# Moving batch 3's loads around batch 2's DMA transpose, and one weight quarter ahead of a load of q

## The chip, the cores and the metric

The kernel runs on one core of one Trainium2 chip. The metric is device time in microseconds (us) of one execution. A verdict calls two kernels the same when they are within 2%; it is unclear when the interval of the ratio reaches past 2%. A run counts as fast when it is at most 1.5% above the fastest of its kernel.

Engines: PE (TensorE matmul), PEld (TensorE weight load), DVE (VectorE), ACT (ScalarE), POOL (GpSimd), SP (SyncE). SP computes nothing here: it issues DMAs, in the traces one after the other in program order. PSUM is the memory into which PE writes.

## The reference, cut to what matters

```python
# q, k, v: (8 batches, 8 heads, 576 positions, 64), float32
q_s = softmax(q over its 64);  k_s = softmax(k over the 576 positions)
kv  = einsum('bhsd,bhse->bhde', k_s, v)           # per head 64 x 64
x   = einsum('bhsd,bhde->bhse', q_s, kv)          # -> 4608 tokens x 512
h   = x @ w_in                                    # 512 -> 2048
out = (h * sigmoid(h)) @ w_out                    # 2048 -> 512
```

The 4608 tokens go through the two large matmuls in 9 chunks: `mm1` (512 to 2048, 16 steps a chunk) and `mm2` (2048 to 512, 16 steps a chunk, four for each quarter of w_out). Attention of the next batch is woven in between: exp and row sum of q, transpose of q, the product `kv`, and `xt`, which multiplies the transposed q by `kv`.

## The kernel before

The order in which each engine gets its instructions is the order in which the Python code makes them. A list of units, one `mm1` or `mm2` step each, is walked, and `plan(u, f)` runs f just before unit u. The traces show SP's issues and DVE's instructions in this order.

```python
def load(b, name, src, ccs=None, eng=nc.sync):       # q, k or v of one batch: 1.18 MB, issued by SP
    ...                                              # two buffers for each of qt, kt, vt
    eng.dma_start(out=st[b][name][:, c, :], in_=x[:, c, :])

def tr_dma(b, eng):                                  # transpose of the normalized exp(q), by DMA
    eng.dma_start_transpose(out=qt_tile(b)..., in_=st[b]["eq"]...)

def kvcopy(b, cc):                                   # DVE: kv / column sums -> kvn; frees kv's PSUM tiles
    ...
def xt(t, cc, ...):                                  # PE: needs kvn (DVE) and qT (the DMA transpose)
    ...

# loads on the GpSimd queue, at the start
load_w1(0); load_w1(1); load_w2(0); load_w1(2)
load(1, "qt", q, eng=nc.gpsimd)
load_w2(1)                                           # second quarter of the output weights
load_w1(3)
load(1, "kt", k, eng=nc.gpsimd); load_w2(2); load(1, "vt", v, eng=nc.gpsimd); load_w2(3)
# ... cut: batch 0 ...

def plan_attn(b, u, sm, vs, tp, ks, ox, eng=nc.gpsimd):
    for cc in range(2):
        plan(u + sm[cc], lambda cc=cc: exp(b, "qt", "eq", cc))                        # ACT
        plan(u + sm[cc] + 1, lambda cc=cc: (qsum(b, cc), qnorm(b, cc, nc.gpsimd)))    # DVE, then POOL
    for cc in range(2):
        plan(u + sm[2 + cc], lambda cc=cc: exp(b, "kt", "ek", cc))
        plan(u + vs[cc], lambda cc=cc: vcast(b, cc, eng))
    plan(u + tp, lambda: tr_dma(b, nc.sync))
    if b == 1:
        plan(u + vs[0] + 1, lambda: load_behind(2))  # q, k, v of batch 2
    if b + 2 < B:
        at_ = u + max(tp, vs[1]) + 1
        plan(at_, lambda: [load(b + 2, *x) for x in (("qt", q), ("kt", k), ("vt", v))])
    # ... cut: kv, kvcopy and xt at ks and ox ...

plan_attn(1, begin[1], (-20, -19, -11, -10), (-6, -5), -12, (-4, -3), (-2, 0), V)
plan_attn(2, begin[2], (-23, -21, -18, -15), (-13, -12), -15, (-10, -7), (-5, -3))
for b in range(3, B):
    plan_attn(b, begin[b], (-40, -36, -32, -28), (-34, -30), -20, (-15, -11), (-7, -4))
```

The softmax here doesn't subtract the row's maximum and nothing guards it: scores larger than these inputs give would overflow.

## Time and profile before

| | before |
|---|---|
| time, median of 3 runs | 292.98 us (292.74 to 295.19) |
| span of the profiled run | 291.8 us |
| PE busy | 279.4 us, 96% |
| DVE, ACT, POOL busy | 53%, 52%, 18% |

From the page: busy time of PE (us, share of the span, instructions), and the granted TensorE clock in 40 slices of 7.3 us (9 is 90% or more of full speed).

```profile
PE 279.4 (96%) x1970; PEld 130.4 (45%) x1970; DVE 153.3 (53%) x308; ACT 152.6 (52%) x250; POOL 52.0 (18%) x44
...
PEclk9999999998899999999999999999999999999998
```

PE is the bottleneck, so only its own idle or slow time is worth anything. The longest of PE's waits (what waited, for what, total us, times, longest) are:

```profile
PE o_1076 L179 <- DMA qT<-eq: 2.1, 1, 2.1
PE wps L302 <- DVE warm L258: 1.2, 1, 1.2
PE ops L233 <- DMA W_59<-in_moe_w_out_dram: 0.9, 1, 0.9
PE o_1077 L179 <- DVE kvn_64 L158: 0.8, 1, 0.8
```

Two of the four are one place. Here is PE's timeline around it (start, duration, engine, line, what, count; in brackets the idle time before and what ended it):

```profile
67.86 0.24 PE L179 MATMUL o_1076<-qT,kvn_63 64*64 64x128 bf16 x2
68.92 0.24 PE L179 MATMUL o_1077<-qT,kvn_63 64*64 64x128 bf16 x2 [0.82 <-DVE kvn_64 L158]
71.28 0.53 PE L179 MATMUL o_1076<-qT,kvn_64 64*64 64x384 bf16 x2 [2.12 <-DMA qT<-eq]
...
71.75 1.89 PE L233 MATMUL ops<-W_59,GT 128*128 128x512 bf16 x4
73.43 1.47 PE L198 MATMUL hps<-XT,W_58 128*128 128x448 bf16 x4
```

At `xt` of batch 2, PE waits 0.82 us for kvn and then 2.12 us for the transposed q. The next four matmuls of 512 columns take 1.89 us where others take 1.03. The windows view tells why (us, then busy time and instruction count of PE, PEld, DVE, ACT, POOL; granted clock; share of DMA; GB/s). The clock is 0.83 on average over these 10 us; the clock records in the trace say 0.5 for 3.41 us, from 71.1 to 74.5.

```profile
70.00:80.00 10.00, 8.72 (x43) 3.59 (x43) 3.30 (x5) 5.84 (x9) 2.94 (x3) 0.83 0.98 340
```

Why is the transpose late? From POOL's timeline and SP's:

```profile
56.74 4.19 POOL L103 TENSOR_TENSOR eq<-eq,rzq 128x1152 bf16<-128x1152 bf16 x2 [21.84 <-DVE rzq L98]
...
46.31 0.46 SPq L74 DMA_DIRECT2D qt<-in_q_dram  x1
46.86 2.55 SPq L74 DMA_DIRECT2D kt<-in_k_dram  x1
49.46 2.76 SPq L74 DMA_DIRECT2D vt<-in_v_dram  x1
52.27 14.00 SPq L252 DMA_DIRECT2D out_dram<-ost  x8
66.38 3.23 SPq L114 DMA_TRANSPOSE qT<-eq  x1
```

The transpose's input is ready at 60.93, when POOL ends. But SP issues it at 66.38. In front of it stand the three loads of batch 3 (here) and of batch 2 (just before), and eight stores. Their issues do not take their usual half microsecond: k and v take 2.55 and 2.76 us and the stores 14 us, because SP is held until about the time when an earlier load lands: k's issue ends at 49.41, and q of batch 2 is reported landed at 49.82. The last load lands at 65.79. The transpose lands at 71.24, and PE starts at 71.28.

The 0.8 us for kvn has another cause: DVE is busy with a row sum of batch 3 (1.35 us) that stands in front of batch 2's kvn in its list.

```profile
66.81 1.35 DVE L97 TENSOR_REDUCE zq<-eq 128x18 f32<-128x1152 bf16 x1
68.58 0.28 DVE L158 TENSOR_SCALAR kvn_64<-kvps,rz 128x64 bf16<-128x64 f32 x1
```

### The profile page before, as it was taken

The numbers are of one execution on the slowest core, as the hardware profiler recorded it, in microseconds if no ns is written. First come the engines' busy times: TensorE is split into PE (matmuls) and PEld (weight loads), VectorE is DVE, ScalarE is ACT, GpSimd is POOL, SyncE is SP. The second block draws the span as 40 slices with busy tenths as digits, with TensorE's granted clock in tenths as the row PEclk, the third lists the DMA queues.
The fourth block names the chain that finished last, engine by engine and source line by source line (L and its number), as shares of the span: only waits on it lengthen the run. The fifth ranks groups of instructions, "written<-read, shape, count | busy, mean of one in ns | idle before, by whom it ended". The sixth has DMA issues, their size and how long they took to land.

```text
span 291.8 us, 4982 instructions
## 1 busy us (share of the span) xinstructions
PE 279.4 (96%) x1970; PEld 130.4 (45%) x1970; DVE 153.3 (53%) x308; ACT 152.6 (52%) x250; POOL 52.0 (18%) x44
## 2 busy tenths in 40 slices
PE   8899899995999999999999999999999999999992
PEld 3466554442444444444444444444444444444440
DVE  3985754855454565546554655465453444345431
ACT  5675555853663576357635863486325433553330
POOL 0740500262320035003500250025000000000000
PEclk9999999998899999999999999999999999999998
DMA  7999999998949903991299228001800240023006
GB/s 276 289 199 289 315 232 324 392 391 194 395 106 201 398 30 74 197 400 46 63 184 376 92 52 173 2 1 43 185 2 0 49 97 0 0 67 80 0 0 144
DMA packets 38311, 46.39 MB, mean 159 GB/s; under 512 B 18064, under 2 KB 22160, under 8 KB 38288
## 3 DMA queue, kind: packets, MB, share of 16 engines
q1 hardware_dynamic: 33248, 38.35, 45.1%
q0 software_dynamic: 5040, 7.73, 11.8%
q8 instruction: 15, 0.25, 0.4%
q14 instruction: 8, 0.07, 0.1%
HBM read 36.70 MB, written 9.44 MB: 158 GB/s over the span
## 4 chain that ended last, share of the span: by engine, by line
PE 75%; DMA 21%; SPq 1%; POOL 1%; issue 0%; DVE 0%; ACT 0%
PE ops L233 38%; PE hps L198 34%; DMA W_59<-in_moe_w_out_dram 11%; DMA vt<-in_v_dram 8%; DMA qT<-eq 2%; PE kvps L145 2%; POOL W_58 L274 1%; SPq L74 1%; DVE ost L246 0%; PE o_1076 L179 0%; ACT XT L190 0%; SPq L252 0%; PE o_3057 L179 0%; PE o_3033 L179 0%; PE o_2142 L179 0%
## 5 line engine op out<-in xcount | busy, mean ns | idle before, releaser
L214 DVE SCALAR_TENSOR_TENSOR GT<-sg,hps 128x512 bf16<-128x512 f32 (+2 forms) x176 | 99.7, 584 | 120.7 <-ACT sg L206 119.9
L233 PE MATMUL ops<-W_59,GT 128*128 128x512 bf16 x576 | 147.7, 381 | 1.1 <-DMA W_59<-in_moe_w_out_dram 0.9
L198 PE MATMUL hps<-XT,W_58 128*128 128x512 bf16 (+3 forms) x640 | 147.5, 359 | 0.5 <-DVE XT L188 0.2
L206 ACT ACTIVATE sg<-hps 128x512 f32<-128x512 f32 (+3 forms) x160 | 87.8, 554 | 108.8 <-PE hps L198 104.2
L198 PEld LDWEIGHTS <-W_58 128*128 128x128 bf16 x640 | 62.1, 98 | 66.0 <-issue 3.5
L233 PEld LDWEIGHTS <-GT 128*128 128x128 bf16 x576 | 54.8, 98 | 64.2 <-issue 3.8
L103 POOL TENSOR_TENSOR eq<-eq,rzq 128x1152 bf16<-128x1152 bf16 x14 | 29.6, 2118 | 137.2 <-ACT sg L206 99.5
L97 DVE TENSOR_REDUCE zq<-eq 128x18 f32<-128x1152 bf16 x16 | 21.5, 1346 | 4.1 <-ACT eq L83 4.1
L83 ACT ACTIVATE eq<-qt 128x1152 bf16<-128x1152 f32 x16 | 18.5, 1164 | 2.4 <-DMA qt<-in_q_dram 2.4
L83 ACT ACTIVATE ek<-kt 128x1152 bf16<-128x1152 f32 x16 | 18.5, 1158 | 1.0 <-DMA kt<-in_k_dram 1.0
L248 ACT ACTIVATE ost<-ops 128x512 f32<-128x512 f32 x18 | 10.7, 597 | 9.9 <-PE ops L233 8.8
L246 DVE TENSOR_SCALAR ost<-ops 128x512 f32<-128x512 f32 x18 | 12.3, 685 | 5.4 <-PE ops L233 5.4
L302 PE MATMUL wps<-warm 128*128 128x512 bf16 x32 | 10.1, 471 | 1.2 <-DVE warm L258 1.2
L145 PEld LDWEIGHTS <-ek 64*64 64x64 bf16 x576 | 6.2, 107 | 7.1 <-issue 3.8
L90 POOL CAST vaug_61<-vt 128x1152 bf16<-128x1152 f32 x6 | 6.8, 1160 | 0.0
L90 POOL CAST vaug_60<-vt 128x1152 bf16<-128x1152 f32 x6 | 6.8, 1157 | 0.0
L302 PEld LDWEIGHTS <-warm 128*128 128x128 bf16 x32 | 3.5, 116 | 6.1 <-issue 3.3
L157 DVE RECIPROCAL rz<-kvps 128x1 f32<-128x1 f32 x32 | 5.0, 157 | 0.1
L98 DVE RECIPROCAL rzq<-zq 128x18 f32<-128x18 f32 x16 | 4.3, 266 | 0.9
L145 PE MATMUL kvps<-vaug_60,ek 64*64 64x65 bf16 x288 | 4.0, 194 | 0.4 <-ACT vaug_60 L88 0.4
L145 PE MATMUL kvps<-vaug_61,ek 64*64 64x65 bf16 x288 | 3.8, 194 | 0.1
L158 DVE TENSOR_SCALAR kvn_63<-kvps,rz 128x64 bf16<-128x64 f32 x12 | 3.4, 284 | 0.4
(135 smaller groups left out, 74.8 us busy)
## 6 DMA issues: line engine op xcount, KB each, us to landing
out_dram<-ost SPq DMA_DIRECT2D x72, 128.0 KB, 2.3
qt<-in_q_dram SPq DMA_DIRECT2D x6, 1152.0 KB, 6.0
kt<-in_k_dram SPq DMA_DIRECT2D x6, 1152.0 KB, 9.3
vt<-in_v_dram SPq DMA_DIRECT2D x6, 1152.0 KB, 11.6
W_58<-in_moe_w_in_dram POOLq DMA_DIRECT2D x4, 512.0 KB, 9.7
W_59<-in_moe_w_out_dram POOLq DMA_DIRECT2D x4, 512.0 KB, 19.3
qt<-in_q_dram SPq DMA_DIRECT2D x2, 576.0 KB, 4.0
kt<-in_k_dram SPq DMA_DIRECT2D x2, 576.0 KB, 6.8
```

The source lines that it names most:

```text
L83: nc.scalar.activation(out=o, in_=jgd(st[b][src], cc), func=ACT.Exp)
L90: eng.tensor_copy(o, jgd(st[b]["vt"], cc))
L97: nc.vector.reduce_sum(out=st[b]["zq"][:, cc], in_=e, axis=AX.X)
L103: eng.tensor_tensor(out=e, in0=e, in1=r[:, :, :, None].to_broadcast([128, J, 2, D]), op=ALU.mult)
L145: nc.tensor.matmul(out=t[r][g * 64:(g + 1) * 64, 0:E1], lhsT=st[b]["ek"][r * P:(r + 1) * P, j, G * D:(G + 1) * D], rhs=vaug[b % 2][r * P:( ...
L198: nc.tensor.matmul(out=hps[:, 0:size], lhsT=W1[:, c, fb * 128:(fb + 1) * 128], rhs=XT[t][:, c, off:off + size], start=(c == 0), stop=(c == ...
L206: nc.scalar.activation(out=sg[:, 0:size], in_=hps[:, 0:size], func=ACT.Tanh, scale=0.5)
L214: nc.vector.scalar_tensor_tensor(out=GT[g][:, fb, col:col + n], in0=sg[:, h], scalar=1.0, in1=hps[:, h], op0=ALU.add, op1=ALU.mult,)
L233: nc.tensor.matmul(out=OP[t, tb], lhsT=GT[t][:, fc, tb * 128:(tb + 1) * 128], rhs=W2[:, fc, :], start=(fc == 0), stop=(fc == NFB - 1),)
L246: nc.vector.tensor_scalar_mul(out=ost, in0=OP[t, tb], scalar1=0.5)
L248: nc.scalar.activation(out=ost, in_=OP[t, tb], func=ACT.Copy, scale=0.5)
L302: nc.tensor.matmul(out=wps, lhsT=warm[:, 0:128], rhs=warm, start=True, stop=True)
```

## The change

The intent: the loads of batch 3 are begun around batch 2's transpose (q in front, k and v behind it) instead of all in front; batch 3's exponentials and row sums come later, to match; the second quarter of the output weights goes ahead of q of batch 1 on the GpSimd queue, to remove the wait of 0.9 us.

```diff
     load_w1(2)
+    load_w2(1)
     load(1, "qt", q, eng=nc.gpsimd)
-    load_w2(1)
     load_w1(3)
@@ plan_attn
-        if b + 2 < B:
-            at_ = u + max(tp, vs[1]) + 1
-            plan(at_, lambda: [load(b + 2, *x) for x in (("qt", q), ("kt", k), ("vt", v))])
+        else:
+            x = (("qt", q), ("kt", k), ("vt", v))
+            if b + 1 == 3:
+                plan(u + tp - 3, lambda: load(3, *x[0]))
+                plan(u + tp + 1, lambda: [load(3, *y) for y in x[1:]])
+            if b + 2 < B:
+                plan(begin[3] - 31 if b == 2 else u + tp + 1, lambda: [load(b + 2, *y) for y in x])
@@
-    plan_attn(1, begin[1], (-20, -19, -11, -10), (-6, -5), -12, (-4, -3), (-2, 0), V)
-    plan_attn(2, begin[2], (-23, -21, -18, -15), (-13, -12), -15, (-10, -7), (-5, -3))
-    for b in range(3, B):
+    plan_attn(1, begin[1], (-18, -17, -11, -10), (-6, -5), -12, (-4, -3), (-2, 0), V)
+    plan_attn(2, begin[2], (-23, -21, -18, -15), (-14, -13), -15, (-10, -7), (-5, -3))
+    plan_attn(3, begin[3], (-36, -33, -28, -25), (-27, -24), -20, (-15, -11), (-7, -4))
+    for b in range(4, B):
         plan_attn(b, begin[b], (-40, -36, -32, -28), (-34, -30), -20, (-15, -11), (-7, -4))
```

What this does to SP's list: before, it read "three loads of batch 3, eight stores, transpose, three loads of batch 4". Now it reads "eight stores, q of batch 3, transpose, k and v of batch 3, three loads of batch 4". Planning batch 4's loads at a later unit changes nothing: nothing else of SP stands between the two places. One detail of the diff: the casts of v of batch 2 come one unit earlier.

## The prediction

> **What bounds the kernel now.** TensorE: 279.4 of 291.8 us busy (busy times), and the chain of waits is 75% PE. From 76 us to the end it runs without a stall, so only the first 76 us can give anything. There the list of waits and the timeline show: 0.89 us at 29.0 for the second quarter of the output weights (landed 29.88); 0.25 us at 37.5 for the third quarter (landed 37.49); about 0.25 us at 43.7 for the fourth (landed 43.71); and a hole at batch 2's output product: 0.82 us at 68.1 for kvn, because DVE stands in batch 3's 1.35 us row sum, then 2.12 us at 69.2 for the transposed q of batch 2, issued at 66.38 and landed at 71.24. Right after that hole the granted clock is 0.5 for 3.41 us (71.1 to 74.5), where matmuls of 512 columns start 427 ns apart instead of 216: about 1.65 us more. The Trainium skill ("TensorE: Matmul & The Clock Gate", section on the HAM clock gate) says that an idle window of about 3.4 us halves the clock; the trace agrees (about 2.9 us idle of the 3.4 before it, then 3.41 us at half).
>
> **Why the transpose is late.** Its input was ready at 60.9 (last GpSimd normalization). But the sync queue holds six 1.18 MB loads in front of eight stores in front of it. Their issues block (2.5, 2.8 us) and the stores until 66.3; the last load lands only at 65.79.
>
> **What the change does.** No instruction is added or removed. The stores and q of batch 3 now stand in front of the transpose, k and v behind it. Loads of batch 2 should land as now (49.8, 52.8, 55.8), the stores by about 58, q of batch 3 by about 61. The transpose is then issued at about 61 and lands 4.7 to 4.9 us later, near 66, before its use at 67.7. The row sum of batch 3 moves behind kvn. So 0.8 + 2.1 + 1.65 us and small gaps vanish: today the stretch from 67.86 to 75.17 takes 7.3 us, without stalls its matmuls need 2.4 us. Gain 4.9 us, all on the critical path.
>
> k and v of batch 3 should land by about 69 and 72, before their use at about 76; batch 4's loads by about 81.
>
> **The weight quarter.** It should land at about 26, and the wait of 0.89 us at 29 vanishes. But the third quarter's place in the GpSimd queue is unchanged, so it still lands at about 37.5; PE arrives there earlier and waits about 1.2 us. That gain is given back: at most 0.2 us net, from the fourth quarter. q of batch 1 lands near 29.5, its transpose is issued near 37 instead of 34.93 and should still land near 45, just in time for its use at 46.
>
> I subtract 0.3 us for small new ring stalls.
>
> **Predicted:** 292.98 - 4.9 - 0.2 + 0.3 = 288.2 us, range 286.8 to 290.0. Faster by over 2%: 0.13; within 2%: 0.84; slower: 0.03.
>
> **Right if** the wait for the transposed q of batch 2 is gone, the transpose is issued near 61, the granted clock has no half-speed stretch near 71, and the wait for weights moved from 29 to about 36.5 to 37.5 with nearly the same total. **Wrong if** the third quarter lands earlier too (then up to 1 us more, near 2%), if batch 1's transpose lands after 46 (a new wait of up to 2 us, perhaps a half-speed stretch), if the stores still block the sync queue past 61, or if k of batch 3 comes too late for its exponential.

## The result, and the profile after

The changed kernel took 289.5 us (median of 6 runs, 288.79 to 289.9) against 293.94 us for the kernel before (6 runs, 292.74 to 295.21). The ratio is 0.9846, 95% interval 0.9811 to 0.9881. A ratio is the mean time of one kernel's fast runs over that of the other's of the same rounds, so it is not quite the ratio of the medians. In later rounds on one chip (run e10 below) it was 0.9823 (0.9799 to 0.9848). So the gain is 1.5 to 1.8%, clear of noise. The first comparison puts it under 2%; the interval of e10 just reaches 2%, and the recorded verdict there is unclear.

PE's waits in the changed kernel, all of those of 0.6 us or more:

```profile
PE ops L233 <- issue: 1.7, 11, 0.2
PE kvps L145 <- ACT vaug L88: 1.5, 2, 0.8
PE wps L302 <- DVE warm L258: 1.2, 1, 1.2
PE ops L233 <- DMA W<-in_moe_w_out_dram: 1.1, 1, 1.1
PE qtps L126 <- DVE eq L103: 0.6, 1, 0.6
```

The waits for qT and for kvn in the middle are gone. The first line is not a stall: this trace has 1936 matmul records of 1970, and where one is missing a gap of 0.2 us shows. The lines of `kvps` and `qtps` belong to batch 0, before 16 us. The wait for the output weights is still there, as large as before or larger. PE's timeline at the same `xt`, the windows, and SP's timeline:

```profile
68.72 0.41 PE L179 MATMUL o<-qT,kvn 64*64 64x128 bf16 x8
69.29 0.81 PE L233 MATMUL ops<-W,GT 128*128 128x512 bf16 x3 [0.16 <-issue]
69.94 0.92 PE L198 MATMUL hps<-XT,W 128*128 128x448 bf16 x4
70.79 0.41 PE L179 MATMUL o<-qT,kvn 64*64 64x128 bf16 x8
71.13 1.04 PE L233 MATMUL ops<-W,GT 128*128 128x512 bf16 x4
```

```profile
70.00:80.00 10.00, 9.95 (x54) 4.51 (x54) 6.05 (x10) 7.85 (x13) 5.73 (x4) 1.00 1.05 397
```

```profile
47.80 9.62 SPq L252 DMA_DIRECT2D out_dram<-ost  x8
57.52 0.54 SPq L74 DMA_DIRECT2D qt<-in_q_dram  x1
61.82 3.21 SPq L114 DMA_TRANSPOSE qT<-eq  x1
65.12 0.53 SPq L74 DMA_DIRECT2D kt<-in_k_dram  x1
```

The transpose is issued at 61.82, just after POOL's last normalization ends (61.79), so its input sets the time of the issue now, not the loads in front of it in SP's list. It lands at 66.51, and PE needs it at 68.72. On DVE, the row sum of batch 3 no longer stands in front of kvn, whose last part ends at 68.53, also in time. There is no half clock. The stretch from the first matmul of `xt` to the `mm2` step after its second half lasts 71.13 - 68.72 = 2.41 us; before it was 75.17 - 67.86 = 7.31 us. That is 4.90 us.

Outside this stretch the two profiled runs differ by little. From its end to the end of the span it is 216.7 us in both. Before it, the changed kernel is 0.86 us later (68.72 against 67.86). Most of that is chance of the run: the last load of batch 0 landed at 12.70 us against 12.06, before anything that the change touches. 4.90 - 0.86 is 4.04, the difference of the spans (4.0).

### The profile page after: what moved, and what is told of

Its sections match the earlier page's. It is cut to its first block, busy times and chain, and to the rows that moved or that the text cites. A ratio compares the mean times of both kernels' runs of the same rounds, so it can differ in the third digit from the quotient of the medians.

```text
span 287.8 us, 4948 instructions
## 1 busy us (share of the span) xinstructions
PE 273.3 (95%) x1936; PEld 129.5 (45%) x1970; DVE 153.2 (53%) x308; ACT 152.0 (53%) x250; POOL 52.0 (18%) x44
## 4 chain that ended last, share of the span: by engine, by line
PE 82%; DMA 10%; POOL 2%; issue 1%; DVE 1%; SPq 0%; ACT 0%; ACTq 0%
PE ops L233 40%; PE hps L198 38%; DMA W<-in_moe_w_out_dram 8%; DMA vt<-in_v_dram 3%; PE kvps L145 2%; PE o L179 2%; POOL W L274 1%; POOL W L280 1%; DVE ost L246 0%; SPq L74 0%; DVE GT L214 0%; POOL kt L74 0%; POOL qt L74 0%; DVE vaug L90 0%; ACT XT L190 0%
## 5 line engine op out<-in xcount | busy, mean ns | idle before, releaser
L198 PE MATMUL hps<-XT,W 128*128 128x512 bf16 (+3 forms) x633 | 146.4, 358 | 1.2 <-DVE XT L188 0.3
L233 PE MATMUL ops<-W,GT 128*128 128x512 bf16 x550 | 143.0, 379 | 3.6 <-issue 1.7
L198 PEld LDWEIGHTS <-W 128*128 128x128 bf16 x640 | 61.9, 98 | 65.8 <-issue 2.8
L190 ACT CAST XT<-o 128x512 bf16<-128x512 f32 (+3 forms) x36 | 18.4, 565 | 6.5 <-PE o L179 6.5
L90 POOL CAST vaug<-vt 128x1152 bf16<-128x1152 f32 x12 | 13.5, 1159 | 0.0
L302 PE MATMUL wps<-warm 128*128 128x512 bf16 x31 | 8.8, 440 | 1.2 <-DVE warm L258 1.2
L158 DVE TENSOR_SCALAR kvn<-kvps,rz 128x64 bf16<-128x64 f32 x32 | 9.1, 284 | 1.1
L145 PE MATMUL kvps<-vaug,ek 64*64 64x65 bf16 x576 | 7.8, 194 | 1.6 <-ACT vaug L88 1.5
L179 PE MATMUL o<-qT,kvn 64*64 64x320 bf16 (+7 forms) x128 | 7.7, 296 | 0.4 <-DVE kvn L158 0.3
L179 PEld LDWEIGHTS <-kvn 64*64 64x64 bf16 x128 | 2.6, 104 | 7.6 <-issue 4.6
```

The lines of the kernel that those rows point to most:

```text
L90: eng.tensor_copy(o, jgd(st[b]["vt"], cc))
L145: nc.tensor.matmul(out=t[r][g * 64:(g + 1) * 64, 0:E1], lhsT=st[b]["ek"][r * P:(r + 1) * P, j, G * D:(G + 1) * D], rhs=vaug[b % 2][r * P:( ...
L179: nc.tensor.matmul(out=o1[g][r * 64:(r + 1) * 64, a - first:a - first + n], lhsT=kvn[b % 3][h, cc, r, :], rhs=st[b]["qT"][h, col // P:(col ...
L190: nc.scalar.copy(out=x, in_=o1[g][:, 0:size])
L198: nc.tensor.matmul(out=hps[:, 0:size], lhsT=W1[:, c, fb * 128:(fb + 1) * 128], rhs=XT[t][:, c, off:off + size], start=(c == 0), stop=(c == ...
L233: nc.tensor.matmul(out=OP[t, tb], lhsT=GT[t][:, fc, tb * 128:(tb + 1) * 128], rhs=W2[:, fc, :], start=(fc == 0), stop=(fc == NFB - 1),)
```

## The experiments

Eleven kernels ran (e10 is the changed kernel once more), all with five rounds, in three groups: e1 to e4, e5 to e8, and e9 to e11, each on one chip and beside 11 runs of the kernel before. All were correct. Where a ratio is compared with one of another group, only the kernel before links them. The rivals were: the weight part gives some of the gain; the row sums on DVE give it rather than the loads; the half clock is no cost of its own.

### The weight part alone (e1_weights_only)

```diff
 # kernel before, with
+    load_w2(1)
     load(1, "qt", q, eng=nc.gpsimd)
-    load_w2(1)
-    plan_attn(1, begin[1], (-20, -19, -11, -10), ...
+    plan_attn(1, begin[1], (-18, -17, -11, -10), ...
```

> The kernel before with only the weight part of the change: second quarter of the output weights ahead of q of batch 1, and the exponentials of that q two units later. Theory (the start is paced by the GpSimd queue's loads, so the wait only moves): the 0.9 us wait of PE for the second quarter is gone, a wait of about 1.1 to 1.3 us for the third quarter stands in its place (0.25 before), ratio 0.999 to 1.002. Rival (the 0.9 us is really saved): ratio about 0.997, with no new wait for the third quarter.

Measured: ratio 1.0029 (0.9988 to 1.0070). The weight part gives no gain that can be measured. PE's waits:

```profile
PE o L179 <- DMA qT<-eq: 2.3, 1, 2.3
...
PE o L179 <- DVE kvn L158: 1.2, 2, 0.8
PE ops L233 <- DMA W<-in_moe_w_out_dram: 0.6, 1, 0.6
```

The one wait for output weights is now at 37.8 us, for the third quarter (landed 37.72), as expected; it is 0.6 us and not 1.1 to 1.3, because in this run PE began `mm1` about 0.8 us later than in the profile of before. The clock records of this run show half speed for 6.83 us after the hole, two windows of 3.41, where the profile of before has one. That chance differs from run to run, and it matters below.

### The loads without the weight part (e2_loads_only)

```diff
 # changed kernel, with
-    load_w2(1)
     load(1, "qt", q, eng=nc.gpsimd)
+    load_w2(1)
-    plan_attn(1, begin[1], (-18, -17, -11, -10), ...
+    plan_attn(1, begin[1], (-20, -19, -11, -10), ...
```

> The changed kernel with the weight part undone. Theory (all of the gain comes from batch 2's transpose and from the row sums of batch 3): ratio to before 0.983 to 0.986, the same as the whole change; wait of PE for the second quarter 0.9 us as before, third quarter about 0.25 us. Rival (the weight part gives a part of the gain): 0.3% less gain, ratio 0.987 to 0.989.

Measured: ratio 0.9842 (0.9804 to 0.9880), the same as the whole change's. The expected waits for weights were not met in size: the second quarter's did not show in this run (PE began late again), and the third's was 0.6 us. A wait of 0.8 us for the transposed q showed in this run. The trace says why: each DMA here shows 16 completions, and of q of batch 2 fifteen were in by 50.15 us and the last only at 52.05. The k and v behind it carried the lag on (1.8 and 2.4 us); the stores and q of batch 3 were issued later for it, q landed at 67.08 and the transpose at 69.05. So the margin that the change leaves (2.2 us in the profile after) is about as large as such a lag.

### The old plan of batch 3's exponentials and row sums (e3_old_sums)

```diff
 # changed kernel, with
-    plan_attn(3, begin[3], (-36, -33, -28, -25), (-27, -24), -20, (-15, -11), (-7, -4))
+    plan_attn(3, begin[3], (-40, -36, -32, -28), (-34, -30), -20, (-15, -11), (-7, -4))
```

> The changed kernel with the exponentials, row sums and casts of batch 3 planned where they were before; loads stay as changed. Theory (the idle time of 0.8 us for kvn is a cost of its own, and alone it is too short to halve the clock): a wait of PE for kvn of about 0.8 us comes back at batch 2's output product, the granted clock stays 1.0 there, span about 0.9 us longer than the changed kernel, ratio to before 0.987 to 0.989. Rival (any stall at this place also halves the clock): 2.5 us longer, ratio 0.993. Second rival (the wait for kvn was hidden under the later arrival of the transpose only and costs nothing now): ratio as the whole change, 0.985.

Measured: 290.62 us median, ratio 0.9902 (0.9863 to 0.9940). The wait is back, the transpose's is not, and the profiled run keeps the clock at 1.00 here:

```profile
69.61 0.41 PE L179 MATMUL o<-qT,kvn 64*64 64x128 bf16 x6 [0.82 <-DVE kvn L158]
```

The median is 1.1 us above the changed kernel's and 1.3 above that of e2, which ran in the same rounds; 0.9 was expected. The ratio is a little outside the expected range, because two of the six runs were longer (291.56 and 292.25). One of them has a low mean clock, 0.989; whether a stall of 0.8 us alone sometimes halves the clock is not settled by this.

### The row sums alone (e9_sums_only)

```diff
 # kernel before, with
-    for b in range(3, B):
+    plan_attn(3, begin[3], (-36, -33, -28, -25), (-27, -24), -20, (-15, -11), (-7, -4))
+    for b in range(4, B):
```

> The kernel before with only the later plan of batch 3's exponentials, row sums and casts; all loads as before. Theory (the two waits of the hole lie one behind the other in front of the same product, and the later one, the landing of the transpose, sets its end): the wait for kvn is gone, the wait for the transpose grows from about 2 to about 3 us, the half clock comes as before; ratio 0.997 to 1.003. Rival (the 0.8 us for kvn is saved in full): ratio about 0.997 or less, wait for the transpose still about 2.1 us. The two overlap at the edge; the profile's waits decide.

Measured: ratio 1.0014 (0.9983 to 1.0045), and the wait has moved whole into the next one:

```profile
PE o L179 <- DMA qT<-eq: 3.2, 1, 3.2
```

The half clock came as before (3.41 us from 73.74, by the clock records).

Together e3 and e9 show how two waits behind each other are worth different things in different company. The 0.8 us for kvn is worth nothing as long as the transpose comes later, and a little over 1 us as soon as it does not. Only the loads and the row sums together give the whole gain.

### Filling the hole with dummy matmuls (e4_warm_hole, e5_warm_short)

The question was whether the half clock is a cost of its own, caused by PE's idleness. The first try:

```diff
 # kernel before, in xt, ahead of its matmuls
+            if t == 2 and cc == 0:
+                for n in range(14):
+                    nc.tensor.matmul(out=o1[n % 2], lhsT=warm[:, 0:128], rhs=warm)
```

> The kernel before with 14 dummy matmuls of 128 by 512 on the zero tile put ahead of the first half of batch 2's output product, into the PSUM tiles that this product then overwrites (results stay right). They take about 3.0 us at full clock, in the hole in which PE waits for kvn and the transpose; the transpose lands as late as before. Theory (1.65 us of the hole's cost is the half clock that follows it, caused by the idle time alone): no half-clock stretch near 71 to 75, following matmuls of 512 columns 216 ns apart, ratio 0.993 to 0.996. Rival (the matmuls after the hole are slow for another reason, such as the loads that begin at 71): still 427 ns apart, ratio 1.0.

Measured: ratio 0.9986 (0.9952 to 1.0020), so the expected 0.993 to 0.996 was missed, although the half clock was gone (mean clock 0.995 to 0.998 in all six runs, and times within 0.5 us of each other). The edit itself was at fault:

```profile
69.34 2.98 PE L174 MATMUL o<-warm 128*128 128x512 bf16 x13 [0.78 <-DVE kvn L158]
72.25 0.25 PE L182 MATMUL o<-qT,kvn 64*64 64x128 bf16 x4
```

The second dummy waited 0.78 us as well: its PSUM tile was that of kv, which DVE frees together with writing kvn. So the dummies ended at about 72.3 us and were a fixed floor: a run whose transpose landed earlier could not use it. The second try has nine dummies, all into the first tile:

```diff
-                for n in range(14):
-                    nc.tensor.matmul(out=o1[n % 2], lhsT=warm[:, 0:128], rhs=warm)
+                for n in range(9):
+                    nc.tensor.matmul(out=o1[0], lhsT=warm[:, 0:128], rhs=warm)
```

> The run with 14 dummy matmuls again, made shorter: 9 dummies of 128 by 512 (1.94 us at full clock), all into the first PSUM tile, so that none waits for kvn and their end lies before the landing of the transpose. Theory (the hole costs its idle time in every run, and on top of it one window of half clock, 1.7 us, in most runs, two in a few and none in a few, by the place of the hole in the clock gate's windows; this is the spread of the kernel before, 292.3 to 295.8): with the dummies no run has the half clock after the hole, the mean is near that of the runs of before with the highest mean clock (292.4), ratio 0.993 to 0.996, and the spread is well under 1.5 us; the waits for kvn and transpose still last about 1 us together. Rival (half clock is no part of the cost; those runs of before are fast for another reason): ratio 0.998 to 1.0.

Measured: 292.01 us median (291.41 to 292.57), ratio 0.9919 (0.9888 to 0.9951). Timeline and window:

```profile
67.95 2.11 PE L174 MATMUL o<-warm 128*128 128x512 bf16 x9
69.99 0.25 PE L182 MATMUL o<-qT,kvn 64*64 64x128 bf16 x4
71.79 0.36 PE L182 MATMUL o<-qT,kvn 64*64 64x384 bf16 x4 [1.55 <-DMA qT<-eq]
72.08 1.04 PE L236 MATMUL ops<-W,GT 128*128 128x512 bf16 x4
```

```profile
70.00:80.00 10.00, 8.45 (x53) 3.84 (x53) 3.31 (x5) 6.30 (x10) 3.86 (x3) 1.00 1.03 345
```

The transpose lands as late as before (71.75), PE still idles 1.55 us for it, and the kernel is 2.4 us faster (294.39 - 292.02, means of the same rounds). That is more than was expected (0.993 to 0.996), and the wait is longer than the 1 us expected; the interval, 1.4 to 3.3 us, holds the 1.7 us of one window. The profiles give it more directly: from the landing of the transpose to the `mm2` step at 75.17 (here 74.15) took 3.93 us before and takes 2.40 us now. So the half clock is a cost of its own, and it goes when PE's idle time is filled. It also fits the spread of the kernel before. Of its 34 runs whose clock is listed, four have a mean clock of 0.996 and took 292.3 to 292.6 us; 24 have 0.990 to 0.993, mean 294.3 us; six have 0.981 to 0.987, mean 295.5 us. That is what none, one, and two or more windows of half speed would give: one costs half of 3.41 us, 1.7 us. The mean clock is only a hint, since it counts half speed at the start and the end too; the changed kernel's runs have 0.991 to 0.999 with no such steps in time.

The kept traces show how chance can enter. In all of them, a stretch of full or half clock between two changes lasts a whole multiple of 3.413 us (the kernel before: 64.85 = 19 x 3.413, 3.41, 215.04 = 63 x 3.413). So the clock changes only on a grid of 3.41 us, and the grid lies differently in each run: half clock begins at 71.12 in the kernel before, at 70.40 in e1 and at 73.74 in e9. By these traces it matters how much of the hole falls between two grid lines. PE was idle for 2.77 us of the 3.41 us ahead of the drop in the kernel before, 2.4 us in e9, 1.98 us in e1. In e1 the line cut the hole: 1.16 us of idle time lay behind it, and the clock stayed at half for a second window. A line nearer the middle could leave both parts too short and cost nothing; that would be the four fast runs, but none of them was traced.

### How much may stand in front of the transpose (e6_two_front, e7_none_front)

```diff
 # e6: changed kernel, with q and k of batch 3 in front
-                plan(u + tp - 3, lambda: load(3, *x[0]))
-                plan(u + tp + 1, lambda: [load(3, *y) for y in x[1:]])
+                plan(u + tp - 3, lambda: [load(3, *y) for y in x[:2]])
+                plan(u + tp + 1, lambda: load(3, *x[2]))
 # e7: with none in front
-                plan(u + tp - 3, lambda: load(3, *x[0]))
-                plan(u + tp + 1, lambda: [load(3, *y) for y in x[1:]])
+                plan(u + tp + 1, lambda: [load(3, *y) for y in x])
```

> The changed kernel with q and k of batch 3 in front of batch 2's transpose instead of q alone. Theory (the transpose comes as late as the last bytes queued in front of it; one load more is 1.18 MB, about 3 us): the transpose lands near 69.5 instead of 66.5, 0.5 to 2 us after its use is due at 68.7; ratio 0.987 to 0.992. Rival (only the input of the transpose, ready at 61.8, and the order of the row sums matter, so a second load in front is harmless): lands near 66.5, ratio 0.985.

> The changed kernel with all three loads of batch 3 behind batch 2's transpose. Theory (the transpose's issue is now set by its input at 61.8, so taking the last load away from its front gains nothing; q of batch 3 lands near 69.5 to 70, just before its first exponential at about 70.3): transpose lands near 66 or a little earlier, no wait for it, ratio 0.984 to 0.987, as the changed kernel. Rival (the load of q in front still costs): faster, ratio under 0.983. Second rival (q comes too late): ACT waits for q of batch 3 and PE behind it, ratio 0.988 or more.

Measured: e6 0.9894 (0.9856 to 0.9932), e7 0.9828 (0.9795 to 0.9861). SP's timeline and PE's wait in e6:

```profile
59.38 0.51 SPq L74 DMA_DIRECT2D kt<-in_k_dram  x1
62.07 6.73 SPq L114 DMA_TRANSPOSE qT<-eq  x1
```

```profile
PE o L179 <- DMA qT<-eq: 1.6, 1, 1.6
```

In e6 the transpose's issue begins as soon as its input is there (62.07), but takes 6.73 us instead of 3.21, and it lands at 70.81, 1.96 us behind k (68.85). So being issued in time is not enough: the bytes queued in front count. In e7 the transpose lands at 66.47, practically as in the changed kernel (66.51), and no PE wait for it shows. Its ratio, 0.9828, is below the 0.984 to 0.987 expected and by the letter in the range of the rival (under 0.983), but its interval holds both; e10 and e11 below, which ran in the same rounds as each other, find no difference. Read as PE's wait for the transpose where no row sum is in the way, the dose is: three loads in front 3.2 us (e9), two 1.6 us, one none (0.8 us in e2, with the lagging load), none no wait. Leaving q in front costs nothing in the medians and is not needed; it takes away margin, as e2 shows.

### A try for a faster start (e8_third_ahead)

```diff
 # changed kernel, with
+    load_w2(2)
     load(1, "kt", k, eng=nc.gpsimd)
-    load_w2(2)
-    plan_attn(1, begin[1], (-18, -17, -11, -10), (-6, -5), -12, (-4, -3), (-2, 0), V)
+    plan_attn(1, begin[1], (-18, -17, -9, -8), (-6, -5), -12, (-4, -4), (-2, 0), V)
```

> A try for a faster version: the changed kernel, and also the third quarter of the output weights ahead of k of batch 1, the exponentials of that k two units later, and both halves of the kv product of batch 1 ahead of the fourth quarter's matmuls. Theory (the start is paced by the sum of the loads): the 1.1 us wait for the third quarter is gone, PE then waits for the fourth quarter (lands at about 44.2) or for batch 1's transpose (46.2); at most 0.7 us of gain, ratio 0.982 to 0.985. Rival (each quarter's wait is a cost of its own): 1.1 us or more, ratio 0.981 or less.

Measured: 289.97 us, ratio 0.9859 (0.9822 to 0.9895): no gain over the changed kernel, somewhat outside the expected range. The wait for weights is gone and stands elsewhere:

```profile
PE o L179 <- DMA qT<-eq: 1.4, 1, 1.4
...
PE kvps L145 <- DVE vaug L90: 0.6, 1, 0.6
```

That is now the transpose of batch 1, which took 9.5 us from issue to landing (38.09 to 47.62) beside the GpSimd loads. But fifteen of its 16 completions were in by 46.07, and the last came 1.55 us later, so this profile's wait of 1.4 us is that lag and need not be in the other runs. The six times show no gain, which fits a start paced by the sum of what must be loaded; that this is the reason is not shown.

### The changed kernel again, and the least change (e10_changed_again, e11_none_front_old_weights)

e10 is the changed kernel unedited. e11 is e7 with the weight part undone as in e2.

> The changed kernel once more, on the same chip and in the same rounds as the next. Expected: ratio 0.982 to 0.987, no wait for batch 2's transpose or at most 1 us, no half clock near 70.

> The changed kernel with all loads of batch 3 behind batch 2's transpose and with the weight part undone: the candidate with the least change. Theory (neither the weight part nor q in front of the transpose is worth anything): the same as the changed kernel of these rounds within 0.4%, ratio to before 0.981 to 0.987. Rival (the weight part is worth 0.3%): slower than it by about 0.9 us.

Measured on one chip in the same rounds: e10 289.39 us, 0.9823 (0.9799 to 0.9848); e11 289.37 us, 0.9820 (0.9795 to 0.9845). They are equal, so the weight part and the place of q together are worth nothing that can be measured, and e1 and e2 say the same of the weight part alone. No version that beats the changed kernel was found.

In e10's profile the clock was at half speed from 16.4 to 19.8 us, at the start of `mm1`, and the run (span 287.7 us) was no longer than the first profile's (287.8): PE then had no wait for weights. It used up slow clock where it would otherwise have waited, which fits a start paced by the loads. The profiles of e6 and e7 have the same stretch of half clock (from 16.70 and 16.67 us), each after 3.41 us in which PE was idle for only about 1.5 us or less, with many small matmuls of 64 rows in it. Other profiles had as much idle time there and no drop (1.44 us in e1), so idle time is not all that counts; what else does is not shown.

## Why the prediction was right

The prediction was 288.2 us (286.8 to 290.0), within 2% with a chance of 0.84. Measured were 289.5 and, later, 289.39 us. Against the kernel before of the same rounds the gain was 4.4 us by medians the first time and 5.1 the second; 4.8 was predicted. Point by point:

- **The bottleneck and the place.** Right. All of the gain lies in one stretch of the profile, 4.90 us as predicted. That it fits so well is in part luck: the profile before was of a run with one window of half clock, and none or two would have made it 1.7 us less or more. The stretch without stalls was put at 2.4 us and measured 2.41.
- **Why the transpose was late.** Right: with the loads out of its way it was issued at 61.82 (61 predicted) and landed at 66.51 (near 66). e6 and e7 show that the loads in front were the cause.
- **Landings of the loads.** The order was right, the times too early. The stores landed at 59.5 (58 predicted), q of batch 3 at 64.4 (61), k and v at 71.4 and 74.4 (69 and 72), batch 4's loads by 84.5 (81). The stores' issue was still held back behind the loads of batch 2. In this profile none of it was late enough to make PE wait; in e2's it cost 0.8 us.
- **The row sum in front of kvn.** Right, and e3 and e9 add that it pays only together with the loads.
- **The half clock.** The mechanism was right (e5). The prediction took it for a fixed 1.65 us, read from one profile. By the mean clocks it varies from run to run: none, one or more windows. That may be why the first gain, the second gain and the profile's differ.
- **The weight quarter.** Right: the wait moved from the second quarter to the third (1.11 us, 37.4 to 38.5 in the profile after), and e1 and e11 show a net worth of nothing. The 0.2 us granted to the fourth quarter did not show. Batch 1's transpose landed at 46.21, by the letter past the 46 at which the prediction feared a new wait; none came, since PE reached its use only at 46.94.
- **New ring stalls of 0.3 us.** They did not come: behind the stretch the two spans are equal within 0.1 us.
- **The level.** The range was built around 292.98 us, a median of three runs. The kernel before has a median of 293.9 to 294.5 us in all later rounds, so the predicted time was about 1 us low at the same gain.

The Trainium skill was of use at two places. "TensorE: Matmul & The Clock Gate", section "What's actually happening", says that a free-running window of 3413 ns decides between full and half clock; the traces agree: every stretch of half clock that begins and ends inside a span lasted 3.41 us or, in e1, 6.83, and the clock changes on a grid of 3.413 us that lies differently in each run. "DMA: Bandwidth & Descriptors", section "Queues, rings and completion order", says that each DMA engine consumes one queue's descriptors in ring order; the traces agree: before the change the loads of batch 2, q and k of batch 3 land 3.0 us apart in the order of their issue (49.82 to 61.85), and in e6 the transpose lands 1.96 us after the load in front of it, though its issue had begun 8.7 us before its landing.

## What to carry to other kernels

When a small, urgent DMA shares an in-order queue with bulk loads, compare the time at which its input is ready with the time at which it is issued and lands. Here what was queued in front of it decided, and it was enough to move so much that its input became the limit. Before you count on removing a wait, look at which wait comes next in the same place: here a weight load and a row sum each gave their time straight to the next wait. And count a PE stall of about 3 us as more than its length: here the clock behind it was halved in most runs, at 1.7 us a window, which also widened the spread of the times.

## What the Trainium skill lacked or had wrong

- "TensorE: Matmul & The Clock Gate": its table lets the half clock begin after an idle window of about 3.4 us. Here less than a whole window was enough: two stalls of 0.82 and 2.12 us with 0.24 us of matmuls between them did it in most runs, though not in all (4 of 34 runs show no sign of it). Counted within the 3.41 us of the grid, 1.98 us of idle time (e1), 2.24 us (e6, as PE ended) and more were followed by half clock; 1.55 us (e5), 1.64 us (e6) and 1.87 us (e8, as PE ended) were not. So in these traces, with one on either side, the limit lies between 1.87 and 1.98 us, leaving out the first 17 us, where 1.43 us was enough in e7 and 1.44 us was not in e1.
- "DMA: Bandwidth & Descriptors": no section says that the sync queue holds an issue back when four loads of 1.18 MB are under way. Here issues that take about 0.5 us took 2.55 and 2.76 us, each ending 0.4 to 0.6 us before an earlier load was reported landed.
- The same page, section "Latency and other measured facts", says that two of the DMA engines are usually slower and puts it, as a best guess, to the software (GpSimd) queue alone. In e2 the last of 16 completions of a load on the hardware queue came 1.9 us behind the fifteenth (52.05 against 50.15 us), and the next two loads lagged by 1.8 and 2.4 us, when the GpSimd queue had nothing left after 43.9 us. Which engine it was, the trace does not tell, so this does not settle the guess.
- The same page gives no time for a transpose from issue to landing, alone or beside other loads (only a bandwidth, in "Latency and other measured facts"). Here 128 x 2304 elements of bfloat16 took 4.7 us (median), and 6.5 to 11.2 us for batch 1's transpose beside the GpSimd loads, over all thirteen profiles.
